# Keys, queries and decays of a gated linear attention turned in runs of 32 and 16 rows a head

## The chip, the core and the metric

The kernel runs on one core of one Trainium2 chip. The metric is the time of one execution on the device in microseconds. The engines named below are PE (TensorE), DVE (VectorE), ACT (ScalarE), POOL (GpSimd) and SP (SyncE, which issues all DMAs here). Each of them works off its own row of instructions strictly in order and waits where an operand or a buffer is not ready.

## What is computed

Three stages follow one another: a linear attention with a decay per key row, then two feed-forward layers over its output. Cut to what matters:

```python
def _attn_ref(q, k, v, alpha):            # (4, 8, 768, 48): batch, heads, steps, head width
    state = np.zeros((B, H, D, D))
    for t in range(S):
        state = alpha[:, :, t, :, None] * state + einsum('bhd,bhe->bhde', k[:, :, t], v[:, :, t])
        y[:, :, t] = einsum('bhd,bhde->bhe', q[:, :, t], state)

def _moe_ref(x, w_in, w_out, a, b):       # 3072 tokens, 384 -> 2048 -> 384
    h = x @ w_in
    P = a[0] + a[1] * h + a[2] * h * h + a[3] * h * h * h
    Q = 1.0 + abs(b[0]) * abs(h) + abs(b[1]) * h * h
    return (P / (Q + 1e-06)) @ w_out

def _moe2_ref(x, w_in, w_out, g_ln):      # 3072 tokens, 384 -> 1024 -> 384
    h = x @ w_in
    solu = h * softmax(h)                 # over the 1024
    return (layernorm(solu) * g_ln) @ w_out
```

## The kernel before

**Tiling.** The 768 steps are cut into six chunks of 128. A chunk of all batches and heads is done in two halves of two batches each, so there are 12 halves, i = 0 to 11. Within a half the decays are multiplied up along the 128 steps (P) and, from the end backwards, into factors for the keys (R); then the attention of a chunk is a few matmuls: `sc` (keys by queries, line 420), `y` (line 444, from the masked scores, v and the state Sbd) and `u` (line 483, the chunk's addition to the state). The result of `y` is split into a high and a low part on ACT and DVE into the tile `xt` (lines 470 and 471). `u` goes into the PSUM bank that the first part of `y` held, so it waits for the first `xt` step on DVE.

**Preparing a half.** Halves 0 and 1 are turned on PE (`a_turn`). Halves 2 to 11 are turned on DVE by `a_dve`, which this change is about. A raw tile (alpha, k or q: `ra`, `rk`, `rq`) holds one (batch, four heads) group in each 32 partitions, and in a partition 4 heads x 4 steps x 48 numbers. DVE's transpose turns blocks of 32 x 32. `transpose_in` (lines 286 to 297) makes four of them a tensor: rows 0 to 31 of a head's 48 go out whole, and the pieces of 16 that remain are put together in pairs, which gives three blocks (m = 0, 1, 2) for two heads. The results land in `alT` (decays), or in `qk` (keys and queries side by side). Then come the scan P (line 308), the scan R (line 317), the product of keys and R (line 320), and two transposes that turn the keys back into rows of steps (line 324) for `u`. The product of queries and P is on POOL (line 335). `qk` goes to DRAM (`qk_d`, line 337) and comes back as `qks` with a head's 48 rows in consecutive partitions (`a_move_qk`, lines 273 to 277, four loads); the keys go to DRAM as `kb_d` (line 329) and come back as `kns` (line 282, one load). Through this detour the 48 rows of two heads are placed at partitions 0 and 64, as `sc` wants them.

**The work around it.** The first feed-forward layer runs in 96 units (chunk by 128 columns of the 2048): nine matmuls into a PSUM tile `hp` (line 590, three such tiles), a chain of steps on ACT and DVE (lines 595 to 621; the DVE steps of most units are lines 616, 619, 620 and 621, the last of which writes `p` and frees the `hp` tile), a split on ACT and POOL (lines 623, 624), and nine matmuls into `x2p` (line 636) four units later. Weights arrive as 64-bit numbers and are converted by three DVE steps each (`split_w`, lines 535, 538, 539) in the stretch up to some 460 us. The second feed-forward layer begins with the last units and fills the rest (lines 710 to 786).

**What sets the order.** The program is written half by half and unit by unit: in the main loop each unit takes one step of `half_steps`, which prepares half i + 1 beside the matmuls of half i. Hand-made pins (`pin`, `later`) hold some steps behind a given unit. Between those limits a scheduler that goes by its own costs sets the row of each engine when the program is built, so a changed instruction also moves its neighbours. Buffers matter too: `ra` and `rq` share one buffer, `rk` has one, so a load waits until DVE has read the one before.

Of the kernel before, what the change touches and what calls it, by code (L numbers as in the profile page):

```python
# [7 lines left out]
F32 = mybir.dt.float32  # L8
# [5 lines left out]
ALU = mybir.AluOpType  # L14
# [16 lines left out]
def kernel(  # L31
# [121 lines left out]
    def network(fast):  # L153
# [7 lines left out]
        if fast:  # L161
# [10 lines left out]
            nc.vector.memset(zero, 0.0)  # L172
            NB6 = 6
            PER = CH + 1
            QW = 4 * CH + 2
# [28 lines left out]
        class Half:  # L204
            def __init__(self, i):
                if i == 1:
                    t = [borrow(3, 1024 * p, [B, 2 * CH]) for p in range(2)]
                    self.q = [t[p][:, :, :CH] for p in range(2)]
                    self.k = [t[p][:, :, CH:] for p in range(2)]
                    end = ap_.tile([128, B, 2], F32, name="end1")  # L210
                    self.end = [end[:, :, p] for p in range(2)]
                    self.ends = _view(end[:], 0, [[2, B], [1, 2], [0, D]])
                    self.kn = borrow(2, 0, [B * 192 + 16])
                else:
                    self.q = [qks[:, :, CH * p:CH * p + CH] for p in range(2)]
                    self.k = [qks[:, :, 256 + CH * p:256 + CH * p + CH] for p in range(2)]
                    self.end = [qks[:, :, 512 + p] for p in range(2)]
                    self.ends = _view(qks[:], 512, [[QW, B], [1, 2], [0, D]])
# [53 lines left out]

        def a_move_qk(i):
            qk, kb = moved[i]
            for m, i0, n, d0 in ((0, 0, 32, 0), (1, 0, 16, 32), (1, 16, 16, 64), (2, 0, 32, 80)):
                nc.sync.dma_start(out=qks[d0:d0 + n], in_=qk[m].rearrange("b i x -> i b x")[i0:i0 + n])
            yield

        def a_move(i):
            kb = moved.pop(i)[1]  # L280
            v_load(i)
            nc.sync.dma_start(
                out=kns[:, :B * 192].rearrange("p (b x) -> p b x", b=B), in_=kb[:].rearrange("b t x -> t b x")
            )
            yield

        def transpose_in(raw, dst, off, pstep, mstep):
            r0 = raw[:]
            for m, o in ((0, 0), (2, 192 + 16)):
                nc.vector.transpose(  # L290
                    out=_view(dst, off + m * mstep, [[pstep, 2], [1, 4], [4, 32]]),
                    in_=_view(r0, o, [[384, 2], [48, 4], [1, 32]]),
                )
            for p in range(2):
                nc.vector.transpose(
                    out=_view(dst, off + mstep + p * pstep, [[1, 4], [4, 32]]),
                    in_=_view(r0, p * 384 + 32, [[48, 4], [160, 2], [1, 16]]),
                )

        def a_dve(i):  # L300
# [3 lines left out]
            transpose_in(ra, alT[:], 1, 3 * PER, PER)  # L304
# [5 lines left out]
            qk = ap_.tile([128, 3, QW], F32, name="qk", tag="qk")  # L310
            qv = [_view(qk[:], x * 256, [[CH, 2], [QW, 3], [1, CH]]) for x in range(2)]
            end = _view(qk[:], 512, [[1, 2], [QW, 3]])
            nc.vector.tensor_scalar(end, _view(P[:], CH, [[3 * PER, 2], [PER, 3]]), P_MIN, None, ALU.max)
            nc.vector.reciprocal(_view(d2[:], CH - 1, [[3 * PER, 2], [PER, 3]]), end)
# [4 lines left out]
            transpose_in(raws.pop((i, "rk")), qk[:], 256, CH, QW)  # L319
            nc.vector.tensor_tensor(qv[1], qv[1], _view(R, 0, [[3 * PER, 2], [PER, 3], [1, CH]]), ALU.mult)  # L320
# [8 lines left out]
            nc.sync.dma_start(  # L329
                out=kb_d[:].rearrange("b (j r) x -> (b j) (r x)", r=4), in_=R[:, :768]  # L330
            )
            yield
            Pv = _view(P[:], 1, [[3 * PER, 2], [PER, 3], [1, CH]])
            transpose_in(raws.pop((i, "rq")), qk[:], 0, CH, QW)
# [721 lines left out]
```

## Time and profile before

| | |
|---|---|
| time, median of 3 runs | 798.98 us (798.51 to 801.87) |
| span of the profiled execution (its time outside the span is not listed) | 801.4 us |
| PE busy | 737.2 us (92%) |
| DVE busy | 636.9 us (79%) |
| ACT busy | 534.3 us (67%) |
| POOL busy | 364.2 us (45%) |
| granted PE clock, mean | 0.954 of full speed |

Busy shares are means over stages with different limits: the attention's preparation lies between some 40 and 460 us, and behind that PE is never idle until the last output. So the stretches have to be read apart, and within a stretch the wait that ends last. The profile gives a wait to the engine whose signal came last.

### The profile page before, as it was taken

How to read it: one execution, taken by the hardware profiler on the slowest of the kernel's cores; microseconds unless marked ns; L12 is line 12 of the kernel's file. 1: busy time of each engine (PE TensorE's matmuls, PEld its weight loads, DVE VectorE, ACT ScalarE, POOL GpSimd, SP SyncE). 2: the span in 40 equal slices, each digit the busy share in tenths (PEclk: the TensorE clock that was granted, in tenths of full speed). 3: DMA queues.
4: the chain of work that ended last, by engine and by line, in shares of the span. 5: the costliest groups of instructions: out<-in, count | busy, mean ns of one | idle time of the engine just before them, and what ended most of it. 6: DMA issues, size and time to landing. Idle time of an engine off the chain costs nothing. (4 is left out here: it accounts for less than half of the span.)

```text
span 801.4 us, 13903 instructions
## 1 busy us (share of the span) xinstructions
PE 737.2 (92%) x4976; PEld 613.0 (76%) x4976; DVE 636.9 (79%) x1110; ACT 534.3 (67%) x983; POOL 364.2 (45%) x306
## 2 busy tenths in 40 slices
PE   4777969969999989999999999999999999999994
PEld 4666757758777768787777878888888989989994
DVE  5996999989899889979897976567887697777710
ACT  2235758489786978788878889789865564555630
POOL 3235777776655444545553334243233433432430
PEclk9857899989999989999999999999999999999997
DMA  7759356283755475445826260540024354452461
GB/s 165 191 148 257 89 152 162 86 200 107 210 145 152 98 229 141 125 115 170 187 85 152 79 119 2 195 200 0 1 80 99 115 119 117 108 125 61 103 141 49
DMA packets 87279, 101.75 MB, mean 127 GB/s; under 512 B 34464, under 2 KB 63136, under 8 KB 87200
## 3 DMA queue, kind: packets, MB, share of 16 engines
q1 hardware_dynamic: 87200, 100.77, 47.5%
q8 instruction: 41, 0.67, 0.4%
q14 instruction: 38, 0.31, 0.1%
HBM read 60.59 MB, written 27.56 MB: 110 GB/s over the span
## 5 line engine op out<-in xcount | busy, mean ns | idle before, releaser
L590 PE MATMUL hp<-xt,g 128*128 128x512 f32 x864 | 230.1, 409 | 15.2 <-DVE p L621 9.9
L624 POOL TENSOR_TENSOR gl<-p,gh 128x512 fp32r<-128x512 f32 x96 | 131.7, 1373 | 185.0 <-ACT gh L623 111.8
L590 PEld LDWEIGHTS hp<-xt,g 128*128 128x128 f32 x864 | 166.4, 196 | 59.4 <-DVE p L621 15.6
L636 PE MATMUL x2p<-gh,g 128*128 128x512 f32 x576 | 195.6, 396 | 1.1 <-ACT gh L623 1.1
L636 PEld LDWEIGHTS x2p<-gh,g 128*128 128x128 f32 x576 | 108.6, 189 | 27.0 <-ACT gh L623 1.9
L636 PE MATMUL x2p<-gl,g 128*128 128x512 f32 x288 | 113.4, 394 | 0.0
L774 PE MATMUL op<-w2oh,room 128*128 128x384 f32 x384 | 101.8, 339 | 0.3 <-ACT o L783 0.2
L766 POOL TENSOR_TENSOR room<-room,room 128x1024 fp32r<-128x1024 f32 x22 | 53.9, 2451 | 102.9 <-ACT room L765 92.4
L619 DVE SCALAR_TENSOR_TENSOR w<-w,co,hp 128x512 f32<-128x512 f32 x84 | 61.9, 737 | 43.1 <-ACT hp L618 42.6
L710 PE MATMUL h<-w2ih,x 128*128 128x512 f32 x288 | 90.8, 394 | 0.0
L597 ACT ACTIVATE p<-hp,co 128x512 f32<-128x512 f32 x96 | 65.9, 686 | 13.9 <-POOL gl L624 13.5
L618 ACT ACTIVATE hp<-ah 128x512 f32<-128x512 f32 x84 | 50.1, 597 | 36.3 <-DVE p L616 35.6
L598 ACT ACTIVATE w<-ah,co 128x512 f32<-128x512 f32 x96 | 69.4, 723 | 6.9 <-DVE hp L620 5.7
L616 DVE SCALAR_TENSOR_TENSOR p<-p,co,hp 128x512 f32<-128x512 f32 x84 | 61.6, 733 | 14.8 <-ACT p L597 14.3
L774 PEld LDWEIGHTS op<-w2oh,room 128*128 128x128 f32 x384 | 70.1, 188 | 1.9 <-ACT o L783 0.5
L595 ACT ACTIVATE ah<-hp 128x512 f32<-128x512 f32 x96 | 56.7, 591 | 15.9 <-PE hp L590 15.7
L623 ACT ACTIVATE gh<-p 128x512 fp32r<-128x512 f32 x96 | 59.8, 623 | 9.7 <-DVE p L621 3.4
L774 PE MATMUL op<-w2ol,room 128*128 128x384 f32 x192 | 65.0, 339 | 0.0
L636 PEld LDWEIGHTS x2p<-gl,g 128*128 128x128 f32 x288 | 54.3, 189 | 11.9 <-issue 0.6
L710 PEld LDWEIGHTS h<-w2ih,x 128*128 128x128 f32 x288 | 53.9, 188 | 11.7
L621 DVE SCALAR_TENSOR_TENSOR p<-p,co,hp 128x512 f32<-128x512 f32 x84 | 62.0, 738 | 1.0
L617 ACT ACTIVATE ah<-w,co 128x512 f32<-128x512 f32 x84 | 60.6, 721 | 1.3
(168 smaller groups left out, 1278.0 us busy)
## 6 DMA issues: line engine op xcount, KB each, us to landing
room<-room SPq DMA_DIRECT2D x96, 128.0 KB, 2.3
qk_d<-qk SPq DMA_DIRECT2D x10, 771.0 KB, 4.4
st<-in_moe_w_in_dram SPq DMA_DIRECT2D x15, 512.0 KB, 4.9
st<-in_moe_w_out_dram SPq DMA_DIRECT2D x20, 384.0 KB, 3.6
qks<-qk_d SPq DMA_DIRECT2D x20, 257.0 KB, 5.5
x<-x_d SPq DMA_DIRECT2D x18, 256.0 KB, 3.3
out_dram<-o SPq DMA_DIRECT2D x96, 48.0 KB, 1.6
ra<-in_alpha_dram SPq DMA_DIRECT2D x44, 96.0 KB, 3.4
```

The costliest lines, as they stand in the source:

```text
L590: last["PE", u] = nc.tensor.matmul(hp, lhsT=w[:, kt, 128 * o:128 * o + 128], rhs=xts[c][:, kt, xx, :], start=(kt == 0 and w is hi and xx = ...
L597: nc.scalar.activation(p, hp, AF.Square, bias=co[:, 7:8])
L598: nc.scalar.activation(w, ah, AF.Square, bias=co[:, 6:7])
L616: nc.vector.scalar_tensor_tensor(p, p, a1, hp, ALU.add, ALU.mult)
L617: nc.scalar.activation(ah, w, AF.Ln, bias=rest)
L619: nc.vector.scalar_tensor_tensor(w, w, rest, hp, ALU.add, ALU.mult)
L621: fin[u] = nc.vector.scalar_tensor_tensor(p, p, a0, hp, ALU.add, ALU.mult)
L623: last["ACT", u] = nc.scalar.activation(gh, p, AF.Copy)
L624: last["POOL", u] = nc.gpsimd.tensor_tensor(gl, p, gh[:].bitcast(F32), ALU.subtract)
L636: nc.tensor.matmul(x2ps[c][d], lhsT=w[:, o, 128 * d:128 * d + 128], rhs=gg, start=(f == 0 and w is hi and gg is gh), stop=(f == NF1 - 1 an ...
L710: nc.tensor.matmul(hp[:, 512 * n:512 * n + 512], lhsT=x2s[c][:, kt, x, CH * b:CH * b + CH], rhs=w2[w][:, kt, 512 * n:512 * n + 512], start ...
L774: nc.tensor.matmul(op, lhsT=x[:, 128 * f:128 * f + 128], rhs=w2[w][:, f, :], start=(f == 0 and x is hi and w == "oh"), stop=(f == NF2 - 1 ...
```

## The change

A head's 48 rows are cut as 32 and 16, the same way for every head. `qk` becomes six blocks of 257 columns (128 queries, 128 keys, one end value): blocks 0 to 3 hold rows 0 to 31 of the four heads, blocks 4 and 5 the remaining 16 rows of two heads each. So a tensor takes one transpose of 512 columns and one of 256 in place of two of 256 and two of 128; the step of four elements on the write side stays. The keys are read back consecutively (128 steps in a row, in place of every fourth step), in one transpose of 512 columns and two of 128; the order of the steps that results is undone by the load of `kns`, which is cut into four loads of 32 partitions. The store of `qk` is cut into three, the load of `qks` into two of 32 rows and four of 16. Scans, products and matmuls keep their sizes.

```diff
+            QB = 2 * CH + 1
+            QW = 2 * QB
...
-                    self.q = [qks[:, :, CH * p:CH * p + CH] for p in range(2)]
-                    self.k = [qks[:, :, 256 + CH * p:256 + CH * p + CH] for p in range(2)]
+                    self.q = [qks[:, :, QB * p:QB * p + CH] for p in range(2)]
+                    self.k = [qks[:, :, QB * p + CH:QB * p + 2 * CH] for p in range(2)]
...
-            for m, i0, n, d0 in ((0, 0, 32, 0), (1, 0, 16, 32), (1, 16, 16, 64), (2, 0, 32, 80)):
-                nc.sync.dma_start(out=qks[d0:d0 + n], in_=qk[m].rearrange("b i x -> i b x")[i0:i0 + n])
+            for j in range(2):
+                nc.sync.dma_start(out=qks[64 * j:64 * j + 32], in_=qk[j].rearrange("b i x -> i b x"))
+            for j in range(2):
+                for p in range(2):
+                    nc.sync.dma_start(
+                        out=qks[64 * j + 32:64 * j + D, :, QB * p:QB * p + QB],
+                        in_=qk[2].rearrange("b i x -> i b x")[16 * p:16 * p + 16, :, QB * j:QB * j + QB],
+                    )
...
-            nc.sync.dma_start(
-                out=kns[:, :B * 192].rearrange("p (b x) -> p b x", b=B), in_=kb[:].rearrange("b t x -> t b x")
-            )
+            for g in range(4):
+                nc.sync.dma_start(
+                    out=kns[32 * g:32 * g + 32, :B * 192].rearrange("j (b x) -> j b x", b=B),
+                    in_=kb[:, :, 192 * g:192 * g + 192].rearrange("b j x -> j b x"),
+                )
...
-        def transpose_in(raw, dst, off, pstep, mstep):
+        def transpose_in(raw, dst, off, step):
             r0 = raw[:]
-            for m, o in ((0, 0), (2, 192 + 16)):
-                nc.vector.transpose(
-                    out=_view(dst, off + m * mstep, [[pstep, 2], [1, 4], [4, 32]]),
-                    in_=_view(r0, o, [[384, 2], [48, 4], [1, 32]]),
-                )
-            for p in range(2):
-                nc.vector.transpose(
-                    out=_view(dst, off + mstep + p * pstep, [[1, 4], [4, 32]]),
-                    in_=_view(r0, p * 384 + 32, [[48, 4], [160, 2], [1, 16]]),
-                )
+            nc.vector.transpose(
+                out=_view(dst, off, [[step, 4], [1, 4], [4, 32]]), in_=_view(r0, 0, [[48, 16], [1, 32]])
+            )
+            nc.vector.transpose(
+                out=_view(dst, off + 4 * step, [[step, 2], [1, 4], [4, 32]]),
+                in_=_view(r0, 32, [[48, 8], [384, 2], [1, 16]]),
+            )
...
-            for p in range(2):
-                nc.vector.transpose(
-                    out=_view(kb, 96 * p, [[32, 3], [192, 4], [1, 32]]),
-                    in_=_view(qk[:], 256 + CH * p, [[QW, 3], [1, 4], [4, 32]]),
-                )
-            kb_d = dram.tile([B, CH, 192], F32, name="kb_d", tag="kb_d", bufs=2)
+            nc.vector.transpose(
+                out=_view(kb, 0, [[48, 4], [192, 4], [1, 32]]), in_=_view(qk[:], CH, [[QB, 4], [1, CH]])
+            )
+            for j in range(2):
+                nc.vector.transpose(
+                    out=_view(kb, 48 * j + 32, [[192, 4], [96, 2], [1, 16]]),
+                    in_=_view(qk[:], QB * (4 + j) + CH, [[1, CH]]),
+                )
+            kb_d = dram.tile([B, 32, 768], F32, name="kb_d", tag="kb_d", bufs=2)
...
-            nc.sync.dma_start(out=qk_d[:].rearrange("m b i x -> (b i) m x"), in_=qk)
+            for j in range(2):
+                nc.sync.dma_start(
+                    out=qk_d[j].rearrange("b i (p x) -> (b i) p x", p=2), in_=_view(qk[:], QB * j, [[QW, 2], [1, QB]])
+                )
+            nc.sync.dma_start(out=qk_d[2].rearrange("b i x -> (b i) x"), in_=_view(qk[:], 2 * QW, [[1, QW]]))
```

The rows of the engines move with it. Lines of the kernel after stand 6 to 11 higher from here on: 619 is 630, 620 is 631, 616 is 627, 621 is 632, 471 is 482, 531 is 542; the key transposes are 329 and 333, the forward ones 298 and 301.

DVE, while half 6 is prepared, from the key transposes to `xt`; before:

```order
L324 STREAM_TRANSPOSE alT<-qk 128x3x4x32 x2
L295 STREAM_TRANSPOSE qk<-rq 128x4x32 x2
L616 SCALAR_TENSOR_TENSOR p<-p,co,hp 128x512
L621 SCALAR_TENSOR_TENSOR p<-p,co,hp 128x512
L290 STREAM_TRANSPOSE qk<-rq 128x2x4x32
L619 SCALAR_TENSOR_TENSOR w<-w,co,hp 128x512
L620 SCALAR_TENSOR_TENSOR hp<-w,hp 128x512
L621 SCALAR_TENSOR_TENSOR p<-p,co,hp 128x512
L471 TENSOR_TENSOR xt<-y,xt 128x2x256
L471 TENSOR_TENSOR xt<-y,xt 128x256
```

and after:

```order
L333 STREAM_TRANSPOSE alT<-qk 128x8x16 x2
L627 SCALAR_TENSOR_TENSOR p<-p,co,hp 128x512
L632 SCALAR_TENSOR_TENSOR p<-p,co,hp 128x512
L298 STREAM_TRANSPOSE qk<-rq 128x4x4x32
L301 STREAM_TRANSPOSE qk<-rq 128x2x4x32
L630 SCALAR_TENSOR_TENSOR w<-w,co,hp 128x512
L631 SCALAR_TENSOR_TENSOR hp<-w,hp 128x512
L627 SCALAR_TENSOR_TENSOR p<-p,co,hp 128x512
L632 SCALAR_TENSOR_TENSOR p<-p,co,hp 128x512
L630 SCALAR_TENSOR_TENSOR w<-w,co,hp 128x512
L482 TENSOR_TENSOR xt<-y,xt 128x2x256
```

The pair of steps 627 and 632 now stands ahead of all query transposes, and the first `xt` step stands behind seven unit steps in place of five.

DVE, while half 7 is prepared, from the product of keys and R; before:

```order
L320 TENSOR_TENSOR qk<-qk,alT 128x2x3x128
L324 STREAM_TRANSPOSE alT<-qk 128x3x4x32 x2
L295 STREAM_TRANSPOSE qk<-rq 128x4x32 x2
L290 STREAM_TRANSPOSE qk<-rq 128x2x4x32
L616 SCALAR_TENSOR_TENSOR p<-p,co,hp 128x512
L619 SCALAR_TENSOR_TENSOR w<-w,co,hp 128x512
L535 TENSOR_SCALAR ft<-st 128x512
L620 SCALAR_TENSOR_TENSOR hp<-w,hp 128x512
L538 SCALAR_TENSOR_TENSOR ft<-st,ft 128x512
L621 SCALAR_TENSOR_TENSOR p<-p,co,hp 128x512
```

and after:

```order
L326 TENSOR_TENSOR qk<-qk,alT 128x6x128
L329 STREAM_TRANSPOSE alT<-qk 128x4x4x32
L333 STREAM_TRANSPOSE alT<-qk 128x8x16 x2
L298 STREAM_TRANSPOSE qk<-rq 128x4x4x32
L301 STREAM_TRANSPOSE qk<-rq 128x2x4x32
L630 SCALAR_TENSOR_TENSOR w<-w,co,hp 128x512
L631 SCALAR_TENSOR_TENSOR hp<-w,hp 128x512
L627 SCALAR_TENSOR_TENSOR p<-p,co,hp 128x512
L632 SCALAR_TENSOR_TENSOR p<-p,co,hp 128x512
L546 TENSOR_SCALAR ft<-st 128x512
```

The conversion steps (535 and 538 before, 546 after) stood ahead of the step that writes `p`, 621, and stand behind its successor 632 now. One short query transpose that stood ahead of the product has gone behind the key transposes.

SP, from the keys' way back in half 2 to the last load of `qks`; before:

```order
L282 DMA kns<-kb_d 128x4x192
L266 DMA ra<-in_alpha_dram 32x4x192 x4
L337 DMA qk_d<-qk 128x3x514
L531 DMA lent_175<-in_moe_w_out_dram 128x384
L531 DMA st<-in_moe_w_in_dram 128x512
L276 DMA qks<-qk_d 32x4x514
L276 DMA qks<-qk_d 16x4x514 x2
L276 DMA qks<-qk_d 32x4x514
```

and after:

```order
L290 DMA kns<-kb_d 32x4x192 x2
L542 DMA lent_175<-in_moe_w_in_dram 128x512
L345 DMA qk_d<-qk 256x1x257 x2
L348 DMA qk_d<-qk 128x514
L290 DMA kns<-kb_d 32x4x192 x2
L542 DMA st<-in_moe_w_out_dram 128x384
L277 DMA qks<-qk_d 32x4x514
L267 DMA ra<-in_alpha_dram 32x4x192
L277 DMA qks<-qk_d 32x4x514
L267 DMA ra<-in_alpha_dram 32x4x192
L542 DMA lent_175<-in_moe_w_out_dram 128x384
L280 DMA qks<-qk_d 16x4x257 x4
```

The three stores stand between two pairs of `kns` loads, and two `ra` loads and a weight load have come between the loads of `qks`.

## Rows read from the trace of the kernel before

**Rows 1.** stretches: us, busy us (x instructions) by engine, PE clock, DMA share, GB/s

```profile
80.00:200.00 120.00, 105.08 (x761) 82.94 (x763) 112.89 (x175) 85.41 (x158) 86.26 (x72) 0.92 0.50 133
200.00:480.00 280.00, 268.33 (x2089) 214.63 (x2080) 249.38 (x403) 224.12 (x406) 135.82 (x120) 0.99 0.55 144
480.00:790.00 310.00, 309.67 (x1621) 269.88 (x1619) 213.98 (x387) 197.11 (x362) 112.44 (x71) 1.00 0.35 97
290.00:295.00 5.00, 3.72 (x9) 2.95 (x10) 4.96 (x9) 3.64 (x7) 1.29 (x1) 0.55 0.45 170
```

**Rows 2.** PE in time: start us, us, line, tile, count [idle before <-releaser]

```profile
77.15 3.94 PE L420 MATMUL sc<-qks 48*128 48x128 f32 x16 [5.25 <-DMA qks<-qk_d]
...
165.15 1.95 PE L483 MATMUL u<-vns,kns 128*64 128x48 f32 x32 [5.58 <-DVE xt L471]
...
204.94 3.85 PE L590 MATMUL hp<-xt,g 128*128 128x512 f32 x15 [0.86 <-DVE p L621]
...
247.96 2.32 PE L590 MATMUL hp<-xt,g 128*128 128x512 f32 x9 [1.88 <-DVE p L621]
...
291.28 4.21 PE L590 MATMUL hp<-xt,g 128*128 128x512 f32 x9 [2.77 <-DVE p L621]
...
340.77 1.14 PE L483 MATMUL u<-vns,kns 128*64 128x48 f32 x32 [1.12 <-DVE xt L471]
...
383.78 1.14 PE L483 MATMUL u<-vns,kns 128*64 128x48 f32 x32 [1.16 <-DVE xt L471]
...
426.64 1.14 PE L483 MATMUL u<-vns,kns 128*64 128x48 f32 x32 [1.48 <-DVE xt L471]
...
467.80 1.14 PE L483 MATMUL u<-vns,kns 128*64 128x48 f32 x32 [0.53 <-DVE xt L471]
```

**Rows 3.** DVE in time, transposes of halves 6 and 7 and of line 750

```profile
244.59 1.62 DVE L324 STREAM_TRANSPOSE alT<-qk 128x384 f32<-128x384 f32 x2
...
281.16 0.64 DVE L290 STREAM_TRANSPOSE qk<-rq 128x256 f32<-128x256 f32 x1
281.63 1.54 DVE L320 TENSOR_TENSOR qk<-qk,alT 128x768 f32<-128x768 f32 x1
283.21 1.70 DVE L324 STREAM_TRANSPOSE alT<-qk 128x384 f32<-128x384 f32 x2
284.83 0.67 DVE L295 STREAM_TRANSPOSE qk<-rq 128x128 f32<-128x128 f32 x2
285.30 0.72 DVE L290 STREAM_TRANSPOSE qk<-rq 128x256 f32<-128x256 f32 x1
...
562.47 1.23 DVE L750 STREAM_TRANSPOSE room<-room 128x1024 f32<-128x1024 f32 x1
563.63 0.66 DVE L620 SCALAR_TENSOR_TENSOR hp<-w,hp 128x512 f32<-128x512 f32 x1
```

**Rows 4.** DVE and PE in time at `xt` and `u`, 250 us

```profile
250.41 1.01 DVE L471 TENSOR_TENSOR xt<-y,xt 128x512 fp32r<-128x512 f32 x2
...
251.34 1.14 PE L483 MATMUL u<-vns,kns 128*64 128x48 f32 x32
```

**Rows 5.** DVE in time, ahead of `p` at 290 us

```profile
288.50 0.86 DVE L535 TENSOR_SCALAR ft<-st 128x512 int32<-128x512 int32 x1 [1.32 <-DMA st<-in_moe_w_in_dram]
...
290.49 0.73 DVE L621 SCALAR_TENSOR_TENSOR p<-p,co,hp 128x512 f32<-128x512 f32 x1
291.14 0.68 DVE L539 SCALAR_TENSOR_TENSOR ft<-st,ft 128x512 int32<-128x512 int32 x1
```

**Rows 6.** SP in time, store and loads of half 2

```profile
64.43 0.39 SPq L337 DMA_DIRECT2D qk_d<-qk  x1
...
71.96 1.74 SPq L276 DMA_DIRECT2D qks<-qk_d  x4
```

**Rows 7.** DMA issues: tiles, count, KB each, median us to landing

```profile
rq<-in_q_dram SPq DMA_DIRECT2D x40, 96.0 KB, 2.3
...
kns<-kb_d SPq DMA_DIRECT2D x10, 384.0 KB, 7.2
```

More of the change, by code (lines that the diff above doesn't have):

```diff
@@ L174, in network @@
             PER = CH + 1
-            QW = 4 * CH + 2
+            QB = 2 * CH + 1
+            QW = 2 * QB
             d1 = ap_.tile([128, NB6 * PER + 1], BF16, name="d1")
@@ L214, in __init__ @@
                 else:
-                    self.q = [qks[:, :, CH * p:CH * p + CH] for p in range(2)]
-                    self.k = [qks[:, :, 256 + CH * p:256 + CH * p + CH] for p in range(2)]
-                    self.end = [qks[:, :, 512 + p] for p in range(2)]
-                    self.ends = _view(qks[:], 512, [[QW, B], [1, 2], [0, D]])
+                    self.q = [qks[:, :, QB * p:QB * p + CH] for p in range(2)]
+                    self.k = [qks[:, :, QB * p + CH:QB * p + 2 * CH] for p in range(2)]
+                    self.end = [qks[:, :, QB * p + 2 * CH] for p in range(2)]
+                    self.ends = _view(qks[:], 2 * CH, [[QW, B], [QB, 2], [0, D]])
                     self.kn = kns
@@ L281, in a_move @@
             v_load(i)
[L282 to L298 removed]
+            for g in range(4):
[3 more added lines that the diff above has]
+                )
+            yield
+        def transpose_in(raw, dst, off, step):
+            r0 = raw[:]
+            nc.vector.transpose(
+                out=_view(dst, off, [[step, 4], [1, 4], [4, 32]]), in_=_view(r0, 0, [[48, 16], [1, 32]])
+            )
+            nc.vector.transpose(
+                out=_view(dst, off + 4 * step, [[step, 2], [1, 4], [4, 32]]),
+                in_=_view(r0, 32, [[48, 8], [384, 2], [1, 16]]),
+            )
         def a_dve(i):
@@ L303, in a_dve @@
             watch(i, ra)
-            transpose_in(ra, alT[:], 1, 3 * PER, PER)
+            transpose_in(ra, alT[:], 1, PER)
             _run(a_load(i, ("rq",)))
@@ L309, in a_dve @@
             yield
[L310 to L314, printed above, removed]
+            qk = ap_.tile([128, NB6, QB], F32, name="qk", tag="qk")
+            qv = [qk[:, :, x * CH:x * CH + CH] for x in range(2)]
+            end = _view(qk[:], 2 * CH, [[QW, 3], [QB, 2]])
+            nc.vector.tensor_scalar(end, _view(P[:], CH, [[2 * PER, 3], [PER, 2]]), P_MIN, None, ALU.max)
+            nc.vector.reciprocal(_view(d2[:], CH - 1, [[2 * PER, 3], [PER, 2]]), end)
             watch_end(i, end)
@@ L318, in a_dve @@
             yield
-            transpose_in(raws.pop((i, "rk")), qk[:], 256, CH, QW)
-            nc.vector.tensor_tensor(qv[1], qv[1], _view(R, 0, [[3 * PER, 2], [PER, 3], [1, CH]]), ALU.mult)
+            transpose_in(raws.pop((i, "rk")), qk[:], CH, QB)
+            nc.vector.tensor_tensor(qv[1], qv[1], _view(R, 0, [[PER, NB6], [1, CH]]), ALU.mult)
             yield
             kb = R[:, :768].rearrange("p (r x) -> p r x", r=4)
-            for p in range(2):
+            nc.vector.transpose(
+                out=_view(kb, 0, [[48, 4], [192, 4], [1, 32]]), in_=_view(qk[:], CH, [[QB, 4], [1, CH]])
+            )
+            for j in range(2):
                 nc.vector.transpose(
-                    out=_view(kb, 96 * p, [[32, 3], [192, 4], [1, 32]]),
-                    in_=_view(qk[:], 256 + CH * p, [[QW, 3], [1, 4], [4, 32]]),
-                )
-            kb_d = dram.tile([B, CH, 192], F32, name="kb_d", tag="kb_d", bufs=2)
-            nc.sync.dma_start(
-                out=kb_d[:].rearrange("b (j r) x -> (b j) (r x)", r=4), in_=R[:, :768]
-            )
+                    out=_view(kb, 48 * j + 32, [[192, 4], [96, 2], [1, 16]]),
+                    in_=_view(qk[:], QB * (4 + j) + CH, [[1, CH]]),
+                )
+            kb_d = dram.tile([B, 32, 768], F32, name="kb_d", tag="kb_d", bufs=2)
+            nc.sync.dma_start(out=kb_d[:].rearrange("b j x -> (b j) x"), in_=R[:, :768])
             yield
-            Pv = _view(P[:], 1, [[3 * PER, 2], [PER, 3], [1, CH]])
-            transpose_in(raws.pop((i, "rq")), qk[:], 0, CH, QW)
+            Pv = _view(P[:], 1, [[PER, NB6], [1, CH]])
+            transpose_in(raws.pop((i, "rq")), qk[:], 0, QB)
             marks[i, 2] = nc.gpsimd.tensor_tensor(qv[0], qv[0], Pv, ALU.mult)
             qk_d = dram.tile([3, B, 32, QW], F32, name="qk_d", tag="qk_d", bufs=2)
-            nc.sync.dma_start(out=qk_d[:].rearrange("m b i x -> (b i) m x"), in_=qk)
+            for j in range(2):
[3 more added lines that the diff above has]
+            nc.sync.dma_start(out=qk_d[2].rearrange("b i x -> (b i) x"), in_=_view(qk[:], 2 * QW, [[1, QW]]))
             moved[i] = (qk_d, kb_d)
```

## The prediction

> **What bounds the kernel now.** I read the stretches first [rows 1]. From 480 us on TensorE (PE) is busy for 309.67 of 310 us, so whatever is won or lost before 480 us reaches the end at its full size, and nothing behind 480 us is touched by the change. From 80 to 200 us VectorE (DVE) is busy for 112.89 of 120 us and PE for 105.08: DVE bounds. From 200 to 480 us PE has 268.33 of 280 and DVE 249.38: PE bounds, with 11.7 us of gaps. Next the PE rows that have an idle time before them [rows 2]. The engine runs its row in order and most gaps end with DVE: either a matmul into hp waits for the last DVE step of an older unit (p, line 621), or u (line 483) waits for xt (line 471), which empties the PSUM bank that u needs. The gap at 77.15 us is another kind: it ends when the load of qks lands. Every gap after 200 us stands just behind the block in which DVE prepares the next half (10 blocks, i = 2 to 11). So what counts is how many DVE microseconds stand in such a block ahead of those two steps.
>
> **Price of a transpose.** I count from one start to the next, since neighbours on DVE overlap. A forward transpose of 256 columns holds DVE for 281.63 - 281.16 = 0.47 us, two of 128 columns for 285.30 - 284.83 = 0.47 us [rows 3]: 1.84 ns a column at both sizes, so no fixed cost per instruction shows. These write with a step of four elements. The two that bring the keys back (line 324) read with that step: 284.83 - 283.21 = 1.62 us for 768 columns, 2.1 ns each [rows 3]. The transpose of line 750 reads and writes runs: 563.63 - 562.47 = 1.16 us for 1024 columns, 1.13 ns each [rows 3].
>
> [...]
>
> **The change, part by part.**
> 1. Forward transposes, three tensors a half: four instructions become two, with the same 768 columns and the same step of four on the write side. By start-to-start 768 x 1.84 = 1.42 us before and after: nothing. If what one lasts beyond its spacing (0.64 - 0.47 = 0.17 us, the row at 281.16 [rows 3]) were all cost, two instructions fewer would save 0.34 a tensor, 1.0 a half. I take 0, since on a full engine the spacing is what counts; 1.0 is the far end, and a loss is not suggested by any row.
> 2. Keys back: 768 columns now read consecutively. At line 750's pace 768 x 1.13 = 0.87 us, so 0.75 less a half. The other end is the forward pace, 1.42 us, 0.2 less, if the short runs of 16 in the new second and third instruction cost as much as a step. I take 0.75: both sides are runs, as on line 750.
> 3. DMA: the store of qk in three pieces (one before), the load of qks in six (four), that of kns in four (one): seven more issues a half. Four loads take SP 1.74 us [rows 6], 0.43 each, so 3 us of SP a half. From half 3 on nobody waits for qks or kns in [rows 2], so 0. For half 2 see point 5.
> 4. The order moves, as the three places in the section on the change show. On DVE the pieces of the query transposes now stand together, and the steps of the units slip around them. Half 6: p of the older unit now stands ahead of all query transposes, which takes 0.75 + 0.47 = 1.2 us off the gap before 247.96. But xt falls behind more unit steps: from the start of the key transposes to the end of the first xt it was 6.5 us (244.59 to about 251.06, the first of the pair at 250.41 [rows 4]), now 0.87 + 1.42 + seven steps of about 0.65 (291.14 - 290.49 [rows 5]) + 0.66 = 7.5. u followed at 251.34, directly on it [rows 4]; PE would come there 1.2 us earlier (250.1) and xt end near 252.1, so u waits about 2 us. With 1.2 off the gap of 1.88, that is 0.8 lost.
>  Half 7: on DVE a weight conversion that waited 1.32 us for its DMA stood ahead of p, line 621, at 290.49 [rows 5]; it now stands behind. From the first step behind the scan (281.16 [rows 3]) to the start of that p there were 9.3 us; now 1.5 (the product at 281.63, which took 1.54 there) + 0.87 + 1.42 + three steps = 5.8, so p would start near 287 and end before 287.8. PE wanted its matmul at 291.28 - 2.77 = 288.5 [rows 2], so the gap of 2.77 us goes.
>  Half 8: two unit steps fall behind xt (1.3 us), and with 0.75 the gap of 1.12 at u goes. Half 10: xt ends 0.3 us later in spite of the saving, and u comes two matmuls sooner: 0.5 lost. Halves 5, 9 and 11 keep their order near xt: 0.75, 0.75 and 0.53 (all there is) off the gaps at 204.94, 383.78 and 467.80.
>  Halves 3 and 4 lie where DVE bounds: 0.75 each, 1.5. The 5.58 us at 165.15 is DVE being late. u now stands 13 matmuls further back there, nine of them into a new hp that DVE has to free first; with DVE late, I count nothing for that.
> 5. Half 2, whose qks PE waits for. DVE should finish the query transposes 2 to 3 us sooner (xt and two conversions stood between them). Against that stand two more stores, two more loads, and two alpha loads and a weight load now between them on SP: seven issues at 0.43, 3 us. The path from the store's issue at 64.43 to the loads' at 71.96 was already 7.5 us [rows 6]. I take 0, with 3 us either way.
>
> **Sum.** Halves 3 and 4: -1.5; 5: -0.75; 6: +0.8; 7: -2.77; 8: -1.1; 9: -0.75; 10: +0.5; 11: -0.53; half 2: 0. Together -6.1 us on a span of 801.4, so 795.3. The profiled execution stands 2.4 us above the median of the three times (798.98), so 792.9 on the median.
>
> Not counted is the clock. [...]
>
> **Rivals.**
> (a) DVE is not what the gaps are made of, or the moves cancel the saving: where DVE gets done sooner it waits for ScalarE instead, and the gaps at u and hp stay. Then only halves 3 and 4 and some of half 7 remain, 2 us: 797 on the median. For it: half 6 and 10 already lose by the order. Against: most of the gaps of [rows 2] end with DVE.
> (b) The saving is larger: the forward transposes give their far end (1.0 a half) and the fall of the clock at half 7 goes. DVE then has 1.75 less a half; the gaps still left take perhaps 5 us of it, and the clock 3: 785.
> (c) Slower: the round trip of half 2 in series. If each of the four added pieces (two stores, two loads) cost its whole landing, 2.3 us for a 96 KB load [rows 7], 9.2 us would be added where PE waits one for one: 795.3 + 9.2 = 804.5 on the span, 802.1 on the median. It decides once PE's gap before the first sc of half 2 passes 5.25 + 6.1 = 11.4 us. Against it: pieces are issued 0.43 apart and not in turn, and the one kns load of 384 KB took 7.2 us to land where quarter-size loads take 2.3 [rows 7]. With a fall of the clock on top, or with unit steps moved badly at two more halves, it would reach 806.
> [...]
> (d) It doesn't do what it says: reads in runs are no faster, and line 750's pace has another cause. Then 0.2 a half is left, with the order's gains and losses: 796 to 799.
>
> **How the numbers follow.** Forecast 0.40 (788 to 795); (a) and (d) together 0.32 (795 to 800); (b) 0.15 (781 to 788); (c) and other losses by the order 0.13 (800 to 808). About 0.5% is what a measurement of this kernel can tell from no change: 795.0 and 803.0. Faster: 0.40 and 0.15, with a little of (a): 0.57. Same: 0.32. Slower: 0.11. The range leaves out the far half of (b) and the worse half of (c): 783 to 802.
>
> **What would show it.** Line 324's successors, 768 columns, at 0.9 us from first start to next (1.4 would be the far end). Forward transposes at 1.42 us a tensor by spacing, though each lasts longer than its spacing. DVE's busy time 80 to 480 us down by 6 us or more. The gap near 291 us gone, a gap at u near 250 us of about 2 us, the gap before the first sc of half 2 between 2 and 8 us. After 480 us the same rows, shifted. I am wrong if PE's gaps between 80 and 480 us stay at 26 us in sum, or if the clock falls in new places and that costs more than DVE saves.

## The result, and the profile after

The changed kernel takes 813.05 us (median of four runs, 809.46 to 815.39), the kernel before 800.42 us beside it. The ratio estimated from all these runs is 1.0136, 95% interval 1.0099 to 1.0173 (the two medians alone would give 1.0158). It is slower, and outside the range that was given (783 to 802).

The stretches of the changed kernel, with the columns of [rows 1]:

```profile
80.00:200.00 120.00, 99.53 (x682) 77.37 (x682) 112.45 (x161) 84.58 (x157) 87.92 (x73) 0.92 0.53 137
200.00:480.00 280.00, 266.48 (x2121) 214.40 (x2122) 245.63 (x368) 219.58 (x399) 126.96 (x120) 0.98 0.54 142
480.00:790.00 310.00, 308.68 (x1606) 267.66 (x1605) 220.66 (x394) 201.81 (x370) 113.01 (x72) 1.00 0.36 97
```

Between 80 and 480 us DVE is busy for a little less (358.1 us against 362.3), but not over the whole execution, where it had 636.9 us before:

```profile
PE 735.6 (91%) x4976; PEld 611.8 (76%) x4976; DVE 638.2 (79%) x1060; ACT 534.0 (66%) x983; POOL 356.0 (44%) x306
```

What the keys' transposes save is taken up by other steps, for instance the first step of the weight conversion (before, then after: twelve instructions of 606 ns and of 918):

```profile
L535 DVE TENSOR_SCALAR ft<-st 128x512 int32<-128x512 int32 x12 | 7.3, 606 | 2.0 <-DMA st<-in_moe_w_in_dram 2.0
```

```profile
L546 DVE TENSOR_SCALAR ft<-st 128x512 int32<-128x512 int32 x12 | 11.0, 918 | 7.7 <-DMA st<-in_moe_w_in_dram 7.7
```

And PE stands still for longer: 20.5 + 13.5 = 34.0 us, where [rows 1] give 14.9 + 11.7 = 26.6. That is 7.4 us, and the profiled execution is 6.2 us longer than that of before (span 807.6 against 801.4). That is half of what the medians differ by: the profiled execution of the changed kernel is the fastest of its four, that of before lies above its median, and what the slower ones lose on top is not in this trace.

What PE waits for between 80 and 480 us; first before, then after (total us, times, longest):

```profile
PE u L483 <- DVE xt L471: 10.7, 6, 5.6
PE hp L590 <- DVE p L621: 9.9, 8, 2.8
PE hp L590 <- DVE p L614: 4.5, 5, 2.5
```

```profile
PE hp L601 <- DVE p L632: 12.8, 7, 3.3
PE hp L601 <- DVE p L625: 12.1, 5, 5.5
PE u L494 <- DVE xt L482: 4.9, 4, 3.1
```

The wait of u for xt is halved, but hp, the first matmul group of a unit, now waits 24.9 us for the last DVE step of an older unit, where it waited 14.4. It isn't the cheaper transposes that halve the first: the changed work in the rows of before (an experiment below) still has 9.6 us of it. Up to unit 20 the two waits only trade places: the 5.58 us of u at 165.15 [rows 2] are gone, hp waits longer there, and the two kernels are all but level. (Lines 601, 494, 482, 632 and 625 are 590, 483, 471, 621 and 614 of before.)

Where it is lost shows when the units are set side by side: the start of a unit's first hp matmul, counted off PE's rows (nine matmuls a unit), as the distance in us to the same unit of before. Two of the experiments below stand beside it.

| unit | before starts at | after | before's work, after's rows | after's work, before's rows |
|---|---|---|---|---|
| 20 | 192.2 | +1.1 | +1.3 | +0.5 |
| 24 | 214.7 | +6.9 | +7.5 | -0.2 |
| 30 | 248.0 | +4.2 | +5.5 | -0.3 |
| 44 | 321.3 | +5.1 | +6.0 | -4.1 |
| 48 | 344.9 | +9.9 | +10.5 | -3.0 |
| 56 | 388.4 | +6.6 | +9.1 | -3.7 |
| 72 | 472.6 | +7.0 | +11.1 | -4.5 |

Two places carry it: units 20 to 24 (5.8 us, where DVE prepares half 5) and units 44 to 48 (4.8 us, half 8). PE's rows at both, and at the place of half 7:

```profile
200.46 2.33 PE L601 MATMUL hp<-xt,g 128*128 128x512 f32 x9 [3.05 <-DVE p L625]
...
212.40 3.89 PE L601 MATMUL hp<-xt,g 128*128 128x512 f32 x9 [1.88 <-DVE p L625]
...
301.35 2.36 PE L601 MATMUL hp<-xt,g 128*128 128x512 f32 x5 [2.75 <-DVE p L632]
...
346.80 1.95 PE L494 MATMUL u<-vns,kns 128*64 128x48 f32 x32 [3.15 <-DVE xt L482]
```

Behind two of these gaps the clock falls as well:

```profile
212.40:216.30 3.90, 3.90 (x10) 3.12 (x11) 2.92 (x5) 2.56 (x5) 1.88 (x2) 0.56 0.70 204
346.80:352.80 6.00, 6.00 (x42) 5.05 (x43) 4.91 (x9) 3.38 (x6) 3.24 (x3) 0.50 1.20 190
```

Nine matmuls into hp take 3.89 us behind 212.40 (clock 0.56) and 2.33 behind 200.46 (1.00).

The transposes themselves did what the change says. DVE where half 7 is prepared, in time:

```profile
288.38 0.71 DVE L329 STREAM_TRANSPOSE alT<-qk 128x512 f32<-128x512 f32 x1
289.02 0.46 DVE L333 STREAM_TRANSPOSE alT<-qk 128x128 f32<-128x128 f32 x2
289.40 1.14 DVE L298 STREAM_TRANSPOSE qk<-rq 128x512 f32<-128x512 f32 x1
290.38 0.68 DVE L301 STREAM_TRANSPOSE qk<-rq 128x256 f32<-128x256 f32 x1
290.88 0.70 DVE L630 SCALAR_TENSOR_TENSOR w<-w,co,hp 128x512 f32<-128x512 f32 x1
...
292.88 0.74 DVE L632 SCALAR_TENSOR_TENSOR p<-p,co,hp 128x512 f32<-128x512 f32 x1
296.97 0.43 DVE L546 TENSOR_SCALAR ft<-st 128x512 int32<-128x512 int32 x1 [3.35 <-DMA st<-in_moe_w_in_dram]
```

The keys' return takes 289.40 - 288.38 = 1.02 us from start to start (1.62 in [rows 3]), a tensor's forward transposes 290.88 - 289.40 = 1.48. The last row is the other side: a weight conversion stands in DVE's row before its DMA has landed, and holds everything behind it for 3.35 us. The 2.75 us gap of PE at 301.35 follows from it.

### The profile page after: what moved, and what is told of

Read it like the earlier page. It is cut to its first block, busy times and chain, and to the rows that moved or that the text cites. A ratio compares the mean times of both kernels' runs of the same rounds, so it can differ in the third digit from the quotient of the medians.

```text
span 807.6 us, 13961 instructions
## 1 busy us (share of the span) xinstructions
PE 735.6 (91%) x4976; PEld 611.8 (76%) x4976; DVE 638.2 (79%) x1060; ACT 534.0 (66%) x983; POOL 356.0 (44%) x306
## 5 line engine op out<-in xcount | busy, mean ns | idle before, releaser
L635 POOL TENSOR_TENSOR gl<-p,gh 128x512 fp32r<-128x512 f32 x96 | 128.3, 1337 | 179.9 <-ACT gh L634 120.6
L608 ACT ACTIVATE p<-hp,co 128x512 f32<-128x512 f32 x96 | 65.8, 686 | 11.7 <-POOL gl L635 11.3
L721 PEld LDWEIGHTS h<-w2ih,x 128*128 128x128 f32 x288 | 53.9, 188 | 11.7
```

What stands on the lines that cost most here:

```text
L608: nc.scalar.activation(p, hp, AF.Square, bias=co[:, 7:8])
L635: last["POOL", u] = nc.gpsimd.tensor_tensor(gl, p, gh[:].bitcast(F32), ALU.subtract)
L721: nc.tensor.matmul(hp[:, 512 * n:512 * n + 512], lhsT=x2s[c][:, kt, x, CH * b:CH * b + CH], rhs=w2[w][:, kt, 512 * n:512 * n + 512], start ...
```

## Experiments

Ratios are to the kernel before in the same job, with 95% intervals.

### One part of the change alone

`keys_only` is the kernel before with only the keys' return changed; in the traces the rows of DVE, ACT and POOL are those of before, and PE's differ in two exchanged pairs of matmuls into y.

```diff
-                    in_=_view(qk[:], 256 + CH * p, [[QW, 3], [1, 4], [4, 32]]),
+                    in_=_view(qk[:], 256 + CH * p, [[QW, 3], [1, CH]]),
...
-            kb_d = dram.tile([B, CH, 192], F32, name="kb_d", tag="kb_d", bufs=2)
+            kb_d = dram.tile([B, 32, 768], F32, name="kb_d", tag="kb_d", bufs=2)
...
+            for g in range(4):
...
```

> The kernel before with the keys' return alone changed: consecutive reads, a linear store, four reordering loads; the forward transposes, the layout and the number of queries' transfers stay. The rows of PE, DVE, ACT and POOL are those of before. Theory A (the loss of after lies in the new row order that the forward part brings, above all in the weight loads that now stand behind the keys' store in SP's row): no loss here, 0.985 to 1.002 of before, line 326's transposes 0.9 us start to start instead of 1.62, about 7 us less busy time of DVE. Rival B (the loss lies in the keys' four loads and the queue time of their issues): 1.01 or more, with waits of u for kns. Rival C (faster reads do nothing, since DVE's time there is hidden): 0.998 to 1.002.

Measured: 0.9972 (0.9938 to 1.0005). Because that left the sign open it ran once more (`keys_again`):

> The kernel before with the keys' return alone changed, once more and with more rounds, since its interval of 0.994 to 1.0005 left open whether it is faster. By the first run 0.995 to 0.999; if DVE's time counted as with the transposes done twice (18.7 us for 16.8 us of work), 6.5 us less would be 0.992.

Measured: 0.9981 (0.9951 to 1.0010). The transposes are cheaper by 6.5 us of busy time in ten halves (the first row is before, the second `keys_only`, up to 500 us):

```profile
L324 DVE STREAM_TRANSPOSE alT<-qk 128x384 f32<-128x384 f32 x20 | 16.8, 883 | 0.1
```

```profile
L326 DVE STREAM_TRANSPOSE alT<-qk 128x384 f32<-128x384 f32 x20 | 10.3, 554 | 0.1
```

The time gains 1.5 to 2.2 us at the middle of the two intervals, and both hold 1. So this part is not the loss, and rival B of the expectation falls.

`fwd_only` is the changed kernel with the keys read in every fourth step again and brought back by one load, still in three transposes:

```diff
-                out=_view(kb, 0, [[48, 4], [192, 4], [1, 32]]), in_=_view(qk[:], CH, [[QB, 4], [1, CH]])
+                out=_view(kb, 0, [[48, 4], [192, 4], [1, 32]]), in_=_view(qk[:], CH, [[QB, 4], [1, 4], [4, 32]])
...
-            kb_d = dram.tile([B, 32, 768], F32, name="kb_d", tag="kb_d", bufs=2)
+            kb_d = dram.tile([B, CH, 192], F32, name="kb_d", tag="kb_d", bufs=2)
...
```

> The changed kernel with the keys' return as before (strided reads, one reordering load in the old form), so the forward part alone: two transposes for four, six blocks of 257, three stores and six loads of queries and keys. Theory A: the loss is here, 1.010 to 1.025 of before, with DVE's waits on the weight loads of 3 us or more in 200 to 350 us and gaps of PE behind them. Rival B (the keys' loads are the cause): 0.995 to 1.003 of before.

Measured: 1.0120 (1.0037 to 1.0203). The loss stays without the consecutive reads: it comes with the rest of the change, which moves rows on every queue.

### Is it the weight loads?

In the changed kernel DVE waits 7.4 us for `st<-in_moe_w_in` between 200 and 350 us. `after_pref` issues each second-layer weight load one tile ahead of its conversion; `before_pref` is the same edit on the kernel before.

```diff
+                while len(ahead) < 2 and x + len(ahead) < len(todo):
...
+                    nc.sync.dma_start(out=raw[:, :s1.shape[1]], in_=s1)
+                    ahead.append(raw)
+                split_w(src, None, keep, scale=scale, raw=ahead.pop(0))
```

> The changed kernel with one edit: the load of a second-layer weight tile is issued one tile ahead of its conversion (two are under way), so that DVE's conversion finds its tile. Theory A: DVE's waits on st<-in_moe_w_in, 7.4 us in 200 to 350 us, fall under 1 us, and the gaps of hp behind them go, 4 to 8 us less than after (0.990 to 0.995 of it). Rival D (the loss is in the order of DVE's row whatever it waits for, for instance xt behind the unit's steps): the waits go, the time stays within 2 us of after.

> The kernel before with the same edit. Theory A: DVE's waits on the weights are only 1.8 us in 200 to 480 us there, so 0 to 3 us less, 0.996 to 1.000. Rival D: the edit moves rows of its own, anything from 0.99 to 1.01.

Measured: `after_pref` 1.0105 (1.0070 to 1.0140), `before_pref` 1.0060 (1.0033 to 1.0087). The wait on `st<-in_moe_w_in` leaves the list of that stretch, 1.0 us for the second layer's other matrix is left, and the time is still 1% over before: theory A, as the whole cause, falls. What DVE no longer waits for the weights it waits elsewhere (xt for ACT, 5.2 us in the same stretch), and over 80 to 480 us hp waits 25.4 us for p.

### The rows of one kernel, the work of the other

To part order from work, a table gives each queue the order in which its instructions issue. `after_in_before` below, with such edges along every queue, is level with before (1.0005), so the edges cost nothing that can be measured there.

```diff
+            for a, b in zip(turn, turn[1:]):
+                tc.add_manual_dep(
+                    made[b], made[a].name,
+                    mybir.DependencyInfo(mybir.DependencyClass.NoSync, mybir.DependencyReason.DATA), reason="rows",
+                )
...
     network(True)
+    rows(TABLE)
```

> The kernel before, every instruction as it was, but with the row order of the changed kernel imposed on all five queues (ordering edges from a table; the four transposes of a tensor stand where the changed kernel's two stand). Theory D (the loss is the row order alone): 1.008 to 1.018 of before, with hp waiting for p (3 us and more) at the places of the changed kernel. Rival E (the loss is in the new work itself: layout with a step of 257, more and smaller transfers): 0.995 to 1.004.

> The changed kernel with the row order of before imposed on all five queues; the queries' transposes alone stand a little later than there, behind the keys' return, where the changed layout holds them. Theory D: the loss goes and the cheaper transposes show, 0.990 to 0.999 of before. Rival E: still 1.008 or more. Of the two, theory D needs both this run fast and the kernel before in the changed order slow.

Measured: `before_in_after` 1.0137 (1.0080 to 1.0193), `after_in_before` 1.0005 (0.9969 to 1.0040). The work of before in the rows of after loses all that after loses, at the same units (the table above) and with the same gaps of PE:

```profile
200.87 2.35 PE L590 MATMUL hp<-xt,g 128*128 128x512 f32 x9 [3.29 <-DVE p L614]
...
213.03 3.90 PE L590 MATMUL hp<-xt,g 128*128 128x512 f32 x9 [2.02 <-DVE p L614]
...
348.60 1.19 PE L483 MATMUL u<-vns,kns 128*64 128x48 f32 x32 [3.72 <-DVE xt L471]
```

In the other direction the loss goes, and hp waits 7.8 + 4.7 us for p:

```profile
PE u L494 <- DVE xt L482: 9.6, 6, 4.7
PE hp L601 <- DVE p L625: 7.8, 4, 3.2
PE hp L601 <- DVE p L632: 4.7, 5, 1.7
```

The loss is the row order. The new transposes, the layout with its step of 257 and the seven more transfers a half cost nothing that can be measured. The gain that the second expectation hoped for (0.990 to 0.999) does not show in the time either. In the profile it is there up to unit 72 (-4.5 us in the table) and gone at the end (span 802.1 us against 801.4): behind the last matmul into hp PE takes 207.0 us, where it took 201.5 before, with a wait in the last layer that the profile of before doesn't have:

```profile
770.72 0.69 PE L785 MATMUL op<-w2oh,room 128*128 128x384 f32 x1 [2.70 <-ACT room L776]
```

Such a wait comes and goes between executions of one program (last section), so it is not put down to the change.

### How lucky is the order of before?

`before_u18` and `after_u18` begin the second layer's weight conversions two units later, which moves rows and no work:

```diff
-    U2, TP = 16, 0.3
+    U2, TP = 18, 0.3
```

> The kernel before with the second layer's weight conversions begun at unit 18 instead of 16, the same work: a neutral shuffle of rows. If the row order of before is a lucky one among many that a small edit reaches (theory F), 1.004 to 1.012; if orders are about equal in time, 0.998 to 1.002.

> The changed kernel with the same shuffle. Theory F: it falls somewhere else in the same band as the shuffled kernel before, 1.000 to 1.012. If the changed layout itself holds the rows back (the queries' transposes behind the keys' return), it stays at 1.010 to 1.016 whatever the shuffle.

Measured: 1.0042 (1.0015 to 1.0068) and 1.0080 (1.0047 to 1.0114). Either shuffle of before (this one and `before_pref`, which also issues loads earlier) costs 0.4 to 0.6%; the three orders that the scheduler gave the changed work (`after_u18`, `after_pref`, `after`) lie at 0.8, 1.05 and 1.4%. The row order of before is better than these two neighbours, and a small edit leaves it. Two neighbours are few to name a band from.

### Which stretch

`late_rows` keeps the changed kernel's rows up to 184 us and has those of before from there on; `half4_rows` has those of before only from 184 to 222 us, `rest_rows` only from 222 us on. (Half 4 in these expectations is the half that PE works on there; the prediction's blocks go by the half that DVE prepares, which is 5.)

> The changed kernel with its own row order up to 184 us on all queues and the row order of before from there on. By the starts of the units the two orders are level at unit 20 (+1.1 us) and 7 to 10 us apart at unit 48. If the loss comes behind 184 us, as that says: 0.998 to 1.003 of before. If it comes from the first part (halves 2 and 3): 1.008 or more.

> The changed kernel in its own order on all queues but for one stretch, 184 to 222 us (units 19 to 24, half 4), where all five queues have the rows of before. By the starts of the units this stretch costs the changed kernel 5.8 us (level at unit 20, +6.9 at unit 24). If the stretch costs by itself: 1.004 to 1.009 of before, and unit 24 starts within 1.5 us of before's distance at unit 20. If a loss saved here comes back further on: 1.011 to 1.015.

> The changed kernel in its own order up to 222 us on all queues and in the order of before from there on. If the losses of the two stretches add: after's 1.0136 less what half4_rows leaves, about 1.006 to 1.010, with unit 24 still 6 us late and the distance then falling, not growing, at unit 48. If the late stretch is harmless: 1.011 to 1.015.

Measured: 0.9994 (0.9964 to 1.0023), 1.0056 (1.0029 to 1.0082), 1.0051 (1.0019 to 1.0083). Each of the two stretches gives back about 0.8% when it is mended alone, and both together all of it. What changes in the first is seen on SP (after, then `half4_rows`):

```profile
201.44 0.35 SPq L338 DMA_DIRECT2D kb_d<-alT  x1
...
205.14 0.97 SPq L542 DMA_DIRECT2D st<-in_moe_w_in_dram  x2
```

```profile
198.04 0.35 SPq L542 DMA_DIRECT2D st<-in_moe_w_in_dram  x1
...
199.88 0.33 SPq L338 DMA_DIRECT2D kb_d<-alT  x1
```

In the changed order the weight load stands behind the keys' store, which waits 3.1 us for the block on DVE to be done, and behind the loads of `ra`. With the old rows it leaves 7 us sooner, DVE's 4.0 us wait for it between 184 and 225 us is gone, and unit 24 starts 0.7 us ahead of before instead of 6.9 behind.

### Which queue

`mend_one` moves only DVE's 15 rows between 188 and 200 us back to the order of before:

> The changed kernel in its own row order, all queues held to it, but for one place: DVE's 15 rows between 188 and 200 us (units 18 to 22, half 4) stand as in the kernel before, so that the two steps which give unit 20's bank free (lines 624 and 625) come ahead of the P scan instead of behind the R scan and the keys' product. If that place is a cause: PE's wait of 3.05 us at 200 us for p falls under 1 us, and with what hangs on it 2 to 6 us go, 1.006 to 1.011 of before. If the loss is spread evenly over all moved rows: 1.011 to 1.014.

Measured: 1.0150 (1.0088 to 1.0213), nothing gained. DVE's waits between 184 and 225 us show why:

```profile
DVE ft L546 <- DMA st<-in_moe_w_in_dram: 5.1, 1, 5.1
DVE hp L624 <- ACT ah L621: 3.4, 2, 2.1
DVE p L625 <- POOL w L623: 1.1, 1, 1.1
```

The two steps that free the bank stand earlier in DVE's row, but ACT and POOL do theirs when their own rows say, so DVE stands and waits for them; and the weight load still stands behind the keys' store. PE's wait at that place is 3.57 us, not under 1. That place on DVE was my reading of the trace, and by itself it is not the cause.

The other runs give single queues of the changed kernel the rows of before, over the whole program: SP's, PE's, both, and all but PE's.

> The changed kernel with SP's rows alone as in before; the other four queues keep the changed kernel's order. If the moved transfers (the weight loads that now stand behind the keys' store) were what costs: 0.998 to 1.004 of before, DVE's 7.4 us of waits on st<-in_moe_w_in in 200 to 350 us gone. If it is the order of the compute rows: 1.008 to 1.014, as with the loads issued one tile ahead.

> The changed kernel with TensorE's rows alone as in before (a half's y and u stand in other places among the units' products, for instance u behind hp of unit 47 instead of ahead of it); the other four queues keep the changed kernel's order. SP's rows alone gave 1.0089. If TensorE's rows carry the larger rest: 1.002 to 1.008 of before, u's wait of 3.15 us at 347 us under 1.5 us. If DVE's, ACT's and POOL's rows carry it: 1.011 to 1.015.

> The changed kernel with TensorE's and SP's rows as in before, DVE, ACT and POOL in the changed kernel's order. If the shares add: SP's 0.45% and TensorE's share together, 0.998 to 1.005. If the order of DVE's steps is what costs: 1.008 or more.

> The changed kernel with the rows of DVE, ACT, POOL and SP as in before and TensorE's alone in the changed order. If TensorE's rows carry the larger rest: 1.004 to 1.010. If DVE's do: 0.998 to 1.003.

Measured: SP 1.0089 (1.0053 to 1.0125), PE 1.0177 (1.0114 to 1.0241), PE and SP 1.0162 (1.0113 to 1.0212), all but PE 1.0029 (1.0003 to 1.0056). SP's rows, the moved transfers, are about a third of the loss by the middle of the interval; since that interval overlaps the changed kernel's, even this third is not clear of noise. The profile of `sp_rows` shows which part goes. DVE's waits for `st<-in_moe_w_in` between 200 and 350 us fall from 7.4 to 0.4 us, and PE's second wait of the first place, 1.88 us at 212.40, is gone; the first stays:

```profile
199.67 3.66 PE L601 MATMUL hp<-xt,g 128*128 128x512 f32 x9 [3.07 <-DVE p L625]
```

From unit 20 to 24 it loses 3.3 us instead of 5.8. TensorE's rows gain nothing when they are given back alone or with SP's; whether they do harm is not clear, since both intervals overlap the changed kernel's. With all queues but PE given back, 0.29% is left. So most of the loss goes when DVE, ACT, POOL and SP change together. DVE, ACT and POOL were not tried one by one.

### What DVE's time is worth in one order

`keys_twice` is the kernel before, in its own rows, with each of the two transposes of the keys done twice:

```diff
-            for p in range(2):
+            for p in (0, 0, 1, 1):
```

> The kernel before in its own row order, with each of the keys' two return transposes done twice: 8 us more of DVE per half's pair would be 16.8 us more busy time over ten halves, no other row moved. If DVE's time there lies on the path in full: 1.019 to 1.022. If only the part that PE's waits expose counts, by the slope of the run with the consecutive reads (6.5 us less busy, 2.2 us less time): 1.004 to 1.010. If hidden: 0.998 to 1.002.

(The expectation's 8 us a half is a slip; its sum of 16.8 us is 1.68 a half.) Measured: 1.0216 (1.0155 to 1.0277), 17.3 us for 34.6 - 16.8 = 17.8 us more busy time. So more work on DVE there costs in full, while 6.5 us less brought about 2. In the two profiles of `keys_only`, which gain 6.7 and 3.6 us by unit 72, 2.8 us of each comes between units 38 and 40. There PE's gap of 2.77 us [rows 2] stays (2.76 and 2.03 us), but the clock does not fall behind it (1.00 over 200 to 480 us in `keys_only`): nine matmuls take 2.33 us instead of 4.21 (`keys_only`):

```profile
287.52 2.33 PE L590 MATMUL hp<-xt,g 128*128 128x512 f32 x9 [2.76 <-DVE p L621]
```

Why more work costs in full and less gains so little in the median was not settled. Two things bear on it: from 200 to 480 us PE is busy for 96% already [rows 1], which leaves little to gain; and up to unit 72 the gain is there, 6.7 and 3.6 us, but `keys_again` loses most of its own again behind the last matmul into hp (last section).

## Why the prediction was wrong, step by step

**What bounds (right for the loss, not for every gain).** What is lost by 480 us does reach the end: the distance is +7.0 us at unit 72 and at the last unit, and the span is 6.2 us longer. What is won need not reach it: `after_in_before` is 4.5 us ahead at unit 72 and 0.7 us behind at the end. That more work on DVE counted in full was shown by `keys_twice` (17.3 us for 17.8 us of busy time).

**Step 1, forward transposes: right.** 1.48 us by spacing against 1.42. Nothing is gained.

**Step 2, keys back: right in kind, 0.15 us off.** 1.02 us against 0.87 forecast: the one of 512 columns takes 0.64 us and the two of 128 take 0.38, where line 750's pace gives 0.58 and 0.29; in `keys_only`, with two of 384, it is 0.95 (busy 554 ns each against 883). With reads in a step of four elements it was 1.62 us for the same 768 columns [rows 3]. The product of keys and R took back a part: 1367 ns in the changed kernel against 1123, 1302 in the old rows and 1188 in `keys_only`. DVE's busy time fell by 4.2 us between 80 and 480 us, not by 6, and over the whole execution it did not fall (638.2 us against 636.9).

**Step 3, more transfers at no cost: right.** `after_in_before` carries all of them and loses nothing. Against rival (c) the prediction compared single loads, 2.3 us for 96 KB and 7.2 for 384 KB [rows 7]. By whole sets it is open whether parts land sooner: one of the four kns loads of 96 KB takes 4.0 us to land in the changed kernel (5.7 in `keys_only`), but SP issues them over 1.8 to 4.5 us, and from the first issue to the last landing it is 6.8 us in the median (8.0 in `keys_only`), against 7.2 for the one of 384 KB [rows 7]. The parts gain little or nothing in landing; that they cost no time is what `after_in_before` shows.

**Step 4, the order: the step that failed.** It put -6.1 us for halves 3 to 11; the profile shows +7.7 from unit 0 (-0.7) to unit 72.
- Halves 3 and 4 were given -1.5 because DVE bounds there. By unit 20 the distance has grown by 1.8 us instead, half 2 in it: what u no longer waits for xt, hp waits for p.
- Half 5 was given -0.75 because the rows near xt keep their order. It lost 5.8 us (units 20 to 24). What moved there is SP's weight load, the steps that free hp's bank on DVE, ACT and POOL, and some rows of PE. DVE's rows alone give nothing back and all queues' rows give it all; SP's alone take away the second of PE's two waits (in one profile, 3.3 us lost instead of 5.8). How the rest divides in that stretch stays open.
- Half 7 was given -2.77 because the conversion that waits for its DMA fell behind p. It fell behind one p and ahead of the next, and since its load on SP had moved as well, the wait grew from 1.32 us [rows 5] to 3.35: the gap is 2.75 us, as before.
- Half 8 was given -1.1. Its gap at u is 3.15 us instead of 1.12 [rows 2], with the clock at 0.50 behind it; some of that comes back by unit 56.
- Half 6 was named as a loss of 0.8 (half 10, of 0.5, was the only other); between units 24 and 30 the distance shrinks by 2.7 us. Its gap at u is 1.07 us, not 2.

The common fault: I followed each block along DVE's row to xt and to the next p, holding the other queues where they were, and took the gaps of the old order as the list of what can be lost. A new order makes gaps of its own. hp's waits for p, 14.4 us before, were never summed.

**Step 5, half 2: right.** The gap before its first sc is 5.93 us (2 to 8 forecast) against 5.25.

**The clock** was left out of the sum. It falls in new places (0.56 from 212.40 us, 0.50 from 346.80), which the last sentence of the prediction names as what would make it wrong; PE's gaps from 80 to 480 us are 34 us where staying at 26 was the mark. No run shows the 3 us that rival (b) put down for the clock; in `keys_only`, where it does not fall at half 7, nine matmuls took 2.33 us instead of 4.21 and 2.8 us were gained between units 38 and 40.

**Rivals.** (c) came true in sign, not in size (802 to 806 against 813), and not in its mechanism: the round trip of half 2 is innocent. "Unit steps moved badly at two more halves" stood in it as an aside, with a chance that was shared with the round trip. It should have been the slower rival itself.

## What to carry to other kernels

Where a scheduler sets the rows, an edit that changes instruction counts is two changes: the work and a new order. Price the order by itself, by imposing each kernel's rows on the other, before judging the work. When rows move, sum the waits by what ends them over the whole stretch, on every queue: here one queue's better rows alone gave about a third of the loss back (SP's, by the middle of its interval) or nothing (DVE's at one place, PE's), and those of four queues together nearly all. And look at what stands ahead of a load in its queue: here SP issued the weight load at 205.14 us behind the keys' store, which waits for DVE (the changed kernel), and at 198.04 us ahead of it (`half4_rows`).

No version here beats the kernel before clearly: its rows with the consecutive reads (`keys_only`) are the nearest to it, at 0.997 and 0.998 with intervals that hold 1.

## What the runs showed that I had not expected

- The same kernel scatters by more than the consecutive reads are worth: `keys_only` lies between 794.0 and 803.4 us in ten runs. Part of that is behind the change's reach: from the start of the last matmul into hp to the end of PE's work, the profiles of `keys_only` and `keys_again`, one and the same program, show 202.4 and 206.6 us. In the second PE waits for `room`, the last layer's input, and the granted clock is 0.66 from 772 to 780 us, behind that:

```profile
771.28 0.69 PE L774 MATMUL op<-w2oh,room 128*128 128x384 f32 x1 [2.58 <-ACT room L765]
```

```profile
772.00:780.00 8.00, 7.75 (x31) 7.46 (x31) 0.49 (x1) 3.06 (x3) 4.71 (x2) 0.66 0.71 167
```

  Eight of the twenty profiles have such a wait, of 2.3 to 2.7 us, and take 204.5 to 207.0 us there; the other twelve, those of before and after among them, take 201.4 to 202.9. How often the runs without a profile have it is not known, so a few us in a single profile's span, or in a median, can come from there.
- The changed layout seems to tie rows together (argued from the layout, not tried). The q, k and end of a block lie side by side with a step of 257 there, and in all ten halves of the changed kernel both query transposes stand behind the keys' return, also in `after_u18` and `after_pref`; in all ten of before one of the four stands ahead of it. `after_in_before`, which keeps that, is level with before, so this alone costs nothing that can be measured.
- The product of keys and R, over the same 768 columns, takes 1367 ns in the changed kernel and 1302 with the same work in the rows of before (`after_in_before`), so in these two profiles the order alone lengthened a DVE step. By what was not tried.
